# Agent attention and maxout FFN: DMA transposes split in two, head operations with places of their own

## The chip, the cores and the metric

One core of a Trainium2 chip runs the whole kernel. The metric is the device time of one execution in microseconds (us), as a median over runs. A profile of one execution gives the busy time of each engine: PE (TensorE, with its weight loads as PEld), DVE (VectorE), ACT (ScalarE), POOL (GpSimd), and SP (SyncE), which here only issues DMAs.

## The reference

Four batches of 12544 tokens with 128 channels pass through an attention over 49 agents, and what comes out through a feed-forward layer with a maximum of three branches:

```python
a2k = softmax(scale * agents @ k.T)      # 49 x 12544, per batch
agent_v = a2k @ v                        # 49 x 128
q2a = softmax(scale * q @ agents.T)      # 12544 x 49
x = q2a @ agent_v                        # 12544 x 128
h = max(x @ w1, x @ w2, x @ w3)          # 50176 x 768
out = h @ w_out                          # 50176 x 128
```

All inputs and the output are 32-bit floats; the kernel computes in bf16 with 32-bit accumulation.

## The kernel before

**Algebra.** x is never formed. Since x = q2a · agent_v, each branch of the layer is q2a · (agent_v · w). Per batch the kernel computes one matrix G from agent_v: columns C31 hold agent_v·(w3−w1) (for the fifth block of 128 columns, f = FI = 4, w3−w2), columns C21 agent_v·(w2−w1), and the columns from C1O on agent_v·w1·w_out and ones that come with it. The differences of the weights stand in `wall`. With e_q = exp(scale · q · agentsᵀ), a hidden block is relu(e_q·G31) (`relu_first`, L674/677, on ACT), then the maximum of this and e_q·G21 (`max_second`, L685/687, on DVE), and w_out multiplies it on PE (L701) on top of the linear part (L692). The softmax sums are divided out at the end (`out_scale`, L708, DVE).

**Stages.** A row tile has 128 rows. Q is worked in 49 groups of 8 row tiles (s = 0 to 48; the last takes the rests of all four batches). K and V of batch 0 are worked in the head, in 11 groups of 9 tiles (8 in the last); K and V of batch b are worked beside the Q groups of batch b−1, in groups s = 12(b−1)+1 to 12(b−1)+11. Groups 36 to 48 have no K work beside them. At the end of each batch's K work, `k_tail` sums the exponentials (L553), divides (L565/566), multiplies with `wall` (L485) and copies the product from PSUM to G (L574 on DVE, L576 on ACT); this is called the border.

**Turns.** The matmuls want q and k with channels on the partitions, so every tile of them has to be transposed. In the head PE turns k (L365) and DVE copies it (L368). Beside the Q groups, SP turns k by one DMA transpose of all 9 tiles of a group from k_bf to kT (`turn_k`, L502), and q by one DMA transpose of 8 tiles in the groups 12, 24 and 36 to 48 (`turn_by_dma`, L633). In the other Q groups PE turns q (L625) and DVE copies it (L629). GpSimd casts q (L620), k (L494) and v (L498) to bf16 before.

**Order.** Each operation is entered with a number, its place, by `at(key, fn)`, and the sorted list is the program: the order of each engine's instructions is that of the places. A group takes 6 units of place. The tables KEY (steady), LATE (groups from 36 on), OWN (named groups), BORDER (the groups around a border), BATCH0 and BATCH3 (`k_tail`) hold the places. STREAM puts loads, casts and DMA turns 11 units and less ahead of the group that uses them. All loads share 14 buffers (`load_tile`); stores are held back by seven groups, with ten buffers for o_sb. All loads, turns and stores are issued by SP, one after the other.

**The head.** `head` loads K and V tiles of batch 0 in turn; w1 and w3 come (L266) ahead of the last V loads and w2 last, after all of V. `cast_w1` (ACT) and `turn_w1` (L317/318) prepare the linear part, the difference operations (L294) fill `wall`, `warm` (L328) issues matmuls on a unit matrix that nothing reads. `normalise` (L409) makes agent_v from the sums, `product` (L412 to 420) multiplies with C31 of `wall` and copies on ACT, and then with C21 and copies on DVE. The difference C21 is split in two halves of 384 columns, one on DVE and one on GpSimd. `keep_busy` (L788) issues some more unread matmuls in the first groups. w_out is loaded (L270) at the end of the head.

Of the kernel before, what the change touches and what calls it, by code (L numbers as in the profile page):

```python
# [11 lines left out]
AF = mybir.ActivationFunctionType  # L12
# [16 lines left out]
    "s": -2.94209, "ex": -2.10461, "u1": -0.58526, "a1": -0.11108, "u2": 2.13391, "a2": 3.22306,  # L29
    "v1": 3.39126, "u3": 3.76716, "x1": 4.61365, "v2": 4.65907, "u0": 4.68062, "a3": 4.76358,  # L30
    "x2": 4.9054, "a0": 5.15584, "v0": 5.44974, "u4": 5.62746, "x0": 6.09964, "a4": 6.12388,
    "u5": 6.27862, "v3": 6.63325, "a5": 6.82242, "v4": 6.98304, "x4": 6.98433, "lin1": 7.02719,
    "oc12": 7.03328, "sum": 7.23728, "oc10": 7.59283, "x3": 7.74792, "v5": 7.87225, "rec": 8.46283,
    "x5": 9.47889, "oc13": 9.6877, "oc11": 9.69832, "oc14": 10.58762, "oc15": 10.856, "lin0": 10.87306,
    "oc05": 11.17012, "sc1": 11.55345, "oc01": 11.72189, "oc00": 11.77009, "oc03": 11.79963,
    "oc02": 11.90624, "oc04": 11.95959, "sc0": 12.74339, "st": 15.47059,
# [3 lines left out]
        "u2": 0.64554, "u0": 0.6497, "a0": 0.75101, "a2": 0.92875, "sum": 1.27525, "u3": 2.06003,  # L40
        "v0": 2.59116, "x0": 2.68446, "a3": 2.85638, "rec": 2.96325, "u1": 3.03882, "v2": 3.6736,
        "u4": 4.24684, "a1": 4.93475, "x2": 5.01871, "v3": 5.81978, "u5": 5.84299, "a4": 5.908,
        "a5": 6.60823, "x3": 6.61479, "v4": 6.9759, "v5": 7.08557, "x4": 7.15158, "v1": 7.27894,
        "x5": 7.66161, "x1": 7.70792, "lin0": 9.14279, "oc05": 10.43605, "oc00": 10.7932, "oc02": 10.85481,
        "oc03": 11.37967, "oc01": 11.41219, "oc04": 11.66746, "sc0": 11.83826, "lin1": 12.49398,
        "oc10": 12.50239, "oc11": 12.59233, "oc12": 12.77266, "oc13": 12.88978, "oc14": 13.54796,
        "oc15": 13.60373, "sc1": 13.75975, "st": 20.17439,
    },
    1: {
        "qt": -4.60541, "qe": -4.48042, "s": -2.95099, "ex": -1.32724, "ks": 1.62294, "u0": 1.73602,  # L50
        "ke": 2.36058, "sum": 2.56616, "kv": 2.79082, "a0": 2.92319, "ka": 3.26757, "u2": 3.4201,
        "v0": 3.45964, "a2": 3.84717, "u3": 4.22117, "rec": 4.22129, "x0": 4.49406, "a3": 4.56793,
        "u1": 4.62522, "v2": 4.63012, "x2": 4.73195, "a1": 4.86854, "v3": 5.12545, "u4": 5.25359,
        "x3": 5.55542, "ea": 5.62671, "a4": 5.96399, "u5": 6.17953, "a5": 6.26476, "v1": 6.28947,
        "x1": 6.30399, "v4": 6.40498, "v5": 6.63853, "x5": 6.88027, "x4": 7.41578, "lin0": 8.99321,
        "oc00": 9.79175, "oc04": 10.56667, "oc02": 10.75084, "oc03": 11.28772, "oc01": 11.5494,
        "oc05": 11.68913, "sc0": 12.27589, "lin1": 12.53566, "oc13": 12.60573, "oc15": 12.61178,
        "oc10": 12.70709, "oc14": 13.24775, "oc12": 13.54581, "oc11": 13.80424, "sc1": 14.02652,
        "st": 19.02898,
    },  # L60
    34: {
        "qt": -2.58866, "qe": -1.82932, "s": -1.30778, "ex": -1.10174, "ks": 0.14415, "sum": 0.55608,
        "rec": 0.59015, "ke": 0.68278, "u0": 0.7058, "ea": 0.72143, "u2": 1.49989, "a0": 2.15219,
        "v0": 2.18384, "x0": 2.25012, "kv": 2.57078, "a2": 2.84672, "ka": 3.10787, "u3": 3.14749,
        "a3": 3.82134, "u1": 3.94172, "v3": 3.96473, "a1": 4.22804, "x3": 4.34837, "v2": 4.43956,
        "u4": 4.5536, "u5": 4.96643, "a4": 5.32988, "x2": 5.54314, "a5": 6.22364, "v4": 6.22498,
        "v1": 6.372, "x4": 6.51691, "v5": 6.61382, "x1": 6.73976, "x5": 6.95861, "lin1": 8.28778,
        "oc15": 8.36021, "lin0": 8.73553, "oc13": 9.18722, "oc04": 9.72211, "oc14": 10.51955,
        "oc01": 10.73827, "oc02": 10.8464, "oc03": 12.33286, "oc05": 12.39876, "oc00": 12.40014,
        "oc11": 12.72237, "sc0": 13.30654, "oc12": 14.30997, "oc10": 14.62572, "sc1": 14.9543,  # L70
        "st": 25.03309,
    },
    35: {
        "qt": -2.43671, "qe": -1.9414, "s": -1.5744, "ex": -1.28805, "ks": -1.09088, "ke": -0.64495,
        "sum": -0.18909, "kv": -0.10783, "ka": 0.5331, "rec": 0.56684, "u0": 0.82589, "a0": 0.91902,
        "u2": 1.00358, "v0": 1.49877, "x0": 1.58537, "a2": 2.26288, "u3": 2.5102, "v2": 2.57899,
        "x2": 3.98475, "u1": 4.05488, "a3": 4.05504, "v3": 4.37636, "a1": 4.49639, "u5": 4.62208,
        "x3": 4.92789, "a5": 5.44572, "v5": 5.48263, "x5": 5.93851, "u4": 7.30642, "a4": 8.24488,
        "v1": 8.30836, "x1": 8.49394, "lin0": 8.71742, "oc03": 8.91263, "oc02": 9.07857, "v4": 9.24912,
        "x4": 9.32541, "oc00": 9.39236, "oc04": 9.69131, "oc01": 10.88106, "lin1": 10.92225,  # L80
        "oc05": 11.01981, "oc15": 11.13488, "sc0": 11.61665, "oc12": 11.69455, "oc13": 11.87736,
        "oc14": 13.32657, "oc10": 13.37252, "oc11": 13.49981, "sc1": 13.74093, "st": 42.57773,
    },
    36: {
        "s": -4.45673, "ex": -3.49789, "u1": -0.09348, "a1": 2.12897, "u2": 2.20348, "a2": 2.77677,
        "v2": 3.2876, "u0": 3.526, "v1": 3.8727, "x2": 4.34512, "x1": 4.34975, "u3": 4.36198,
        "a0": 4.73186, "a3": 5.00514, "v0": 5.29756, "u4": 5.75498, "x0": 5.91535, "sum": 6.0162,
        "a4": 6.30588, "v3": 6.39331, "x3": 6.48929, "u5": 6.75132, "rec": 7.30888, "a5": 7.33831,
        "v4": 7.78698, "v5": 7.80684, "x5": 7.96407, "x4": 8.12232, "lin1": 9.0675, "oc12": 9.24639,
        "oc14": 9.95322, "oc10": 10.40131, "lin0": 10.43281, "oc04": 10.55626, "oc01": 10.64608,  # L90
        "oc11": 11.24862, "oc15": 12.02168, "oc13": 12.20592, "oc00": 12.38398, "oc03": 12.91102,
        "sc1": 12.98528, "oc02": 14.0029, "oc05": 14.08645, "sc0": 14.96085, "st": 29.7755,
    },
    37: {
        "s": -2.47874, "ex": -1.87009, "u1": -0.70419, "a1": -0.60046, "u2": 2.0221, "a2": 2.21078,
        "v2": 3.56807, "x2": 3.92118, "u0": 4.2218, "v1": 4.32407, "x1": 4.92454, "a0": 5.43373,
        "v0": 5.83985, "u3": 6.06605, "x0": 6.29959, "u5": 6.46966, "v3": 6.48031, "a3": 6.91113,
        "a5": 7.46701, "u4": 7.96938, "sum": 8.00459, "x3": 8.25588, "rec": 8.25634, "v5": 8.35007,
        "lin1": 8.44693, "oc11": 8.49987, "a4": 8.62997, "oc13": 8.8661, "v4": 9.25227, "x5": 9.45205,
        "oc12": 9.91769, "x4": 10.00657, "oc10": 10.0531, "lin0": 10.26202, "oc15": 10.56081,  # L100
        "oc14": 10.87787, "oc04": 10.95601, "oc05": 11.15532, "sc1": 11.49682, "oc01": 11.77199,
        "oc02": 11.78318, "oc00": 11.81904, "oc03": 12.16132, "sc0": 13.17137, "st": 43.83189,
    },
    47: {
        "s": -2.63303, "ex": -1.35705, "u1": -0.72334, "a1": -0.55161, "u2": 2.09887, "a2": 2.6128,
        "v1": 2.71229, "u3": 4.07931, "v2": 4.23837, "a3": 4.51758, "x1": 4.63092, "u0": 4.71212,
        "a0": 5.0718, "x2": 5.13888, "u4": 5.22695, "v0": 5.2509, "x0": 5.96934, "u5": 6.00235,
        "a4": 6.49548, "v3": 6.59342, "v4": 6.61016, "sum": 6.94315, "lin0": 6.95342, "x3": 6.98518,
        "a5": 7.11094, "oc00": 7.22404, "oc02": 7.24709, "v5": 7.29105, "rec": 7.33314, "x4": 7.43763,
        "lin1": 7.62467, "oc03": 7.73819, "oc11": 7.80383, "x5": 7.80889, "oc14": 8.24845, "oc12": 8.30273,  # L110
        "oc04": 8.48507, "oc10": 10.74469, "oc01": 11.20725, "oc05": 11.70935, "sc0": 11.81857,
        "oc15": 11.86159, "oc13": 12.01123, "sc1": 12.03976, "st": 16.08395,
    },
    48: {
        "s": -2.45577, "ex": -1.62439, "u1": -0.82051, "a1": -0.04899, "u2": 1.5047, "v1": 1.68501,
        "a2": 1.84167, "u0": 1.85869, "v2": 2.12726, "a0": 2.96358, "x1": 3.66201, "x2": 3.71048,
# [53 lines left out]
    },  # L170
}
BATCH0 = {
    "red": -0.0796, "tot": 0.34012, "nrm": 0.77389, "p31": 0.90693, "p21": 1.22633,
}
BATCH3 = {
    "red": -1.41636, "tot": -0.09802, "nrm": 0.57786, "p31": 0.95637, "p21": 1.99854,
# [658 lines left out]
```

## Time and profile before

| what | time |
|---|---|
| median of 3 runs | 454.76 us (453.74 to 455.93) |
| the profiled execution | 456.01 us |
| its span (first to last instruction) | 454.2 us |
| PE busy | 433.0 us |
| DVE busy | 404.9 us |
| ACT busy | 398.2 us |
| POOL busy | 169.4 us |
| DMA transposes of k, 9 or 8 tiles | 33, median 1380 ns on SP, 4.1 us to landing |
| DMA transposes of q, 8 tiles | 15, median 1237 ns on SP, 3.1 us to landing |
| first hidden matmul of group 0 (L662) starts | 43.66 us |
| exps of q group 2 start | 58.15 us |
| last output block (L708) starts | 448.64 us |

Times of the trace count from the start of the span. What lies around the span is 1.8 us in the profiled execution. A share of busy time is an average over the head, the batches with K work, and the last 13 groups, which have different limits; therefore the trace is read by stage.

### The profile page before, as it was taken

What the parts mean: (1) busy time and instruction counts of PE and PEld (TensorE: products, weight loads), DVE (VectorE), ACT (ScalarE), POOL (GpSimd) and SP (SyncE); (2) the same over time, 40 slices, a digit from 0 to 9 for tenths busy, and PEclk for the clock granted to TensorE, in tenths of its full rate; (3) what the DMA queues carried; (4) which work ended last, traced back from release to release, by engine and by line L of the source; (5) the groups of instructions that cost most, each with busy time, mean ns of one, the idle gap of its engine ahead of it and who ended that gap; (6) DMA issues with size and microseconds to landing.
All of it is one profiled execution on the core that took longest, in us unless ns stands there. A gap on an engine that the chain in (4) does not pass through costs nothing.

```text
span 454.2 us, 13313 instructions
## 1 busy us (share of the span) xinstructions
PE 433.0 (95%) x5506; PEld 278.0 (61%) x5506; DVE 404.9 (89%) x505; ACT 398.2 (88%) x456; POOL 169.4 (37%) x165
## 2 busy tenths in 40 slices
PE   2878999999999999999999999999999999999995
PEld 2754566666665666666665666666665556565664
DVE  3323899999999999999999999999999999999995
ACT  1655899999999999999988999999988899999983
POOL 4334465555424354465423355554410101011000
PEclk9999999999999999999999999999999999999999
DMA  8998999898879989998899999999667686654933
GB/s 316 412 408 318 258 299 256 282 267 274 226 245 327 289 285 292 304 308 260 250 301 292 293 312 273 308 332 268 185 208 179 183 163 187 175 153 150 348 140 140
DMA packets 83655, 118.86 MB, mean 262 GB/s; under 512 B 57671, under 2 KB 59659, under 8 KB 83595
## 3 DMA queue, kind: packets, MB, share of 16 engines
q1 hardware_dynamic: 83392, 117.92, 86.7%
q8 instruction: 43, 0.70, 0.6%
q14 instruction: 17, 0.14, 0.1%
q10 hardware_dynamic: 203, 0.10, 0.1%
HBM read 78.74 MB, written 25.69 MB: 230 GB/s over the span
## 4 chain that ended last, share of the span: by engine, by line
PE 85%; DMA 8%; DVE 4%; issue 1%; ACT 1%; POOL 0%; DVEq 0%; SPq 0%
PE uv_ps L662 34%; PE o_ps L701 32%; PE o_ps L692 6%; DMA st<-in_k_dram 5%; PE m_ps L639 3%; PE m_ps L625 3%; DVE r L687 2%; DMA st<-in_q_dram 2%; PE m_ps L514 2%; PE m_ps L354 2%; DMA ag_st<-in_agents_dram 1%; PE m_ps L650 1%; PE uv_ps L485 1%; DVE o_sb L708 1%; PE o_ps L788 0%
## 5 line engine op out<-in xcount | busy, mean ns | idle before, releaser
L687 DVE TENSOR_TENSOR r<-uv_ps,a_sb 128x1024 bf16<-128x1024 f32 x245 | 297.5, 1222 | 10.1 <-PE uv_ps L662 5.1
L677 ACT ACTIVATE a_sb<-uv_ps 128x1024 bf16<-128x1024 f32 x245 | 242.9, 1024 | 20.2 <-PE uv_ps L662 17.0
L662 PE MATMUL uv_ps<-e_q,G 49*128 49x512 bf16 (+1 forms) x1248 | 182.5, 369 | 2.5 <-ACT G L420 1.0
L701 PE MATMUL o_ps<-wo_bf,r 128*128 128x128 bf16 x2352 | 179.1, 220 | 0.0
L701 PEld LDWEIGHTS <-r 128*128 128x128 bf16 x2352 | 139.8, 98 | 45.2 <-issue 42.2
L662 PEld LDWEIGHTS <-G 49*128 49x128 bf16 x1248 | 57.2, 93 | 63.4 <-issue 25.4
L620 POOL CAST q_bf<-st 128x1024 bf16<-128x1024 f32 x49 | 50.9, 1040 | 104.1 <-DMA st<-in_q_dram 74.7
L708 DVE TENSOR_TENSOR o_sb<-o_ps,recips 128x512 f32<-128x512 f32 x98 | 67.0, 685 | 2.9 <-PE o_ps L701 1.5
L498 POOL CAST v_bf<-st 128x1152 bf16<-128x1152 f32 (+1 forms) x33 | 37.5, 1137 | 50.3 <-DMA st<-in_v_dram 47.6
L685 ACT ACTIVATE r<-uv_ps 128x1024 bf16<-128x1024 f32 x49 | 50.3, 1026 | 1.3 <-PE uv_ps L662 0.6
L494 POOL CAST k_bf<-st 128x1152 bf16<-128x1152 f32 (+1 forms) x33 | 37.5, 1137 | 35.8 <-DMA st<-in_k_dram 35.7
L674 ACT ACTIVATE uv_ps<-uv_ps 128x1024 f32<-128x1024 f32 x49 | 49.6, 1011 | 0.9 <-PE uv_ps L662 0.6
L526 POOL TENSOR_TENSOR Eacc<-Eacc,e_k 128x441 f32<-128x441 f32 x27 | 27.6, 1024 | 36.2 <-ACT e_k L359 36.2
L692 PE MATMUL o_ps<-G,e_q 128*128 128x256 bf16 x196 | 37.9, 275 | 0.0
L645 ACT ACTIVATE e_q<-m_ps 128x512 bf16<-128x512 f32 x49 | 29.2, 597 | 2.3 <-PE m_ps L639 1.2
L629 DVE COPY qT<-m_ps 128x1024 bf16<-128x1024 bf16 x34 | 23.3, 686 | 3.4 <-PE m_ps L625 3.4
L368 DVE COPY kT<-uv_ps 128x1152 bf16<-128x1152 bf16 (+1 forms) x11 | 8.3, 752 | 17.8 <-PE uv_ps L365 17.8
L692 PEld LDWEIGHTS <-e_q 128*128 128x128 bf16 x196 | 12.1, 97 | 18.3 <-issue 18.1
L625 PE MATMUL m_ps<-ident,q_bf 128*128 128x128 bf16 x272 | 21.2, 222 | 0.2 <-POOL q_bf L620 0.2
L639 PE MATMUL m_ps<-qT,agT 128*64 128x512 bf16 (+1 forms) x104 | 19.9, 389 | 0.6 <-DVE qT L629 0.6
L383 ACT ACTIVATE v_bf<-st 128x1152 bf16<-128x1152 f32 (+1 forms) x11 | 12.2, 1112 | 9.3 <-DMA st<-in_v_dram 9.3
L378 POOL CAST k_bf<-st 128x1152 bf16<-128x1152 f32 (+1 forms) x11 | 12.5, 1137 | 18.3 <-DMA st<-in_k_dram 18.3
(73 smaller groups left out, 231.3 us busy)
## 6 DMA issues: line engine op xcount, KB each, us to landing
st<-in_q_dram SPq DMA_DIRECT2D x48, 512.0 KB, 5.9
out_dram<-o_sb SPq DMA_DIRECT2D x48, 512.0 KB, 5.4
st<-in_k_dram SPq DMA_DIRECT2D x40, 576.0 KB, 5.5
st<-in_v_dram SPq DMA_DIRECT2D x40, 576.0 KB, 8.7
st<-in_k_dram SPq DMA_DIRECT2D x4, 512.0 KB, 4.1
st<-in_v_dram SPq DMA_DIRECT2D x4, 512.0 KB, 6.7
st<-in_moe_w_dram SPq DMA_DIRECT2D x3, 384.0 KB, 11.0
kT<-k_bf SPq DMA_TRANSPOSE x33, 4.1
```

The lines of the kernel that those rows point to most:

```text
L494: nc.gpsimd.tensor_copy(out=d["kb"][:, :n, :], in_=d["k"][:, :n, :])
L498: nc.gpsimd.tensor_copy(out=d["vb"][:, :n, :], in_=d["v"][:, :n, :])
L620: nc.gpsimd.tensor_copy(out=d["qb"], in_=d["q"])
L625: nc.tensor.transpose(t[:, j * P:(j + 1) * P], d["qb"][:, j, :], ident)
L662: nc.tensor.matmul(t[:, h, j0 * P:j1 * P], G[b][h * H:h * H + A, col + f * P:col + (f + 1) * P], d["e"][h * H:h * H + A, j0 * P:j1 * P], s ...
L674: nc.scalar.activation(u, u, AF.Relu)
L677: nc.scalar.activation(a_sb[f], u, AF.Relu)
L685: nc.scalar.activation(r, v_ps[f], AF.Relu)
L687: nc.vector.tensor_tensor(out=r, in0=v_ps[f], in1=a_sb[f], op=ALU.max)
L692: nc.tensor.matmul(t[:, i * 2 * C:(i + 1) * 2 * C], d["e"][:, jj * P:(jj + 1) * P], G[batch[jj]][:, C1O:C1O + 2 * C], start=(i == 0), stop ...
L701: nc.tensor.matmul(t[:, c:c + C], r_sb[f][:, h, jj * P:(jj + 1) * P], wo_bf[:, f, :], start=False, stop=True, skip_group_check=True)
L708: nc.vector.tensor_tensor(out=d["out"][:, j:j + m, :], in0=d["o", o].rearrange("p (j c) -> p j c", c=C), in1=d["r"][:, j:j + m].unsqueeze( ...
```

## The change

Every DMA transpose is issued as two in a row, the first with tile 0 and the second with the rest (tiles 1 to 8, or 1 to 7). In the head, the loads of the weights, the differences, the products and their copies get places of their own in a table HEAD; w2 is loaded in two column parts, 512 to 767 early and 0 to 511 after V; w1 and w3 and the first Q group are loaded earlier in SP's order; the C21 difference of 512 columns is one operation on DVE after `normalise`, and that of the other 256 an earlier one on DVE; w1 is turned after the first hidden matmuls. `product` is divided into the product and its copies, which have places of their own; in `k_tail` the copy on ACT becomes two of 512 columns. The tables LATE, OWN, BORDER, BATCH0 and BATCH3 hold other numbers; KEY and STREAM are unchanged.

```diff
 def turn_k():
     d["kT"] = bf_tile("kT", 3)
-    nc.sync.dma_start_transpose(out=d["kT"][:, :n, :], in_=d["kb"][:, :n, :].rearrange("p j c -> p (j c)"))
+    for j0, j1 in ((0, 1), (1, n)):
+        nc.sync.dma_start_transpose(out=d["kT"][:, j0:j1, :],
+                                    in_=d["kb"][:, j0:j1, :].rearrange("p j c -> p (j c)"))
...
 def turn_by_dma():
     d["qT"] = work.tile([P, GT, P], BF16, tag="qT", bufs=3, name="qT")
-    nc.sync.dma_start_transpose(out=d["qT"], in_=d["qb"].rearrange("p j c -> p (j c)"))
+    for j0, j1 in ((0, 1), (1, n)):
+        nc.sync.dma_start_transpose(out=d["qT"][:, j0:j1, :],
+                                    in_=d["qb"][:, j0:j1, :].rearrange("p j c -> p (j c)"))
...
-def load_w(i):
-    wst[i] = load_tile().rearrange("p j c -> p (j c)")[:, :Dff]
-    nc.sync.dma_start(wst[i], (moe_w1, moe_w2, moe_w3)[i])
+def load_w(i, c0=0, c1=Dff):
+    if i not in wst:
+        wst[i] = load_tile().rearrange("p j c -> p (j c)")[:, :Dff]
+    nc.sync.dma_start(wst[i][:, c0:c1], (moe_w1, moe_w2, moe_w3)[i][:, c0:c1])
...
-def differences_21():
-    difference(nc.vector, C21, 1, 0, slice(0, Dff // 2))
-    difference(nc.gpsimd, C21, 1, 0, slice(Dff // 2, Dff))
+def difference_21(cols):
+    difference(nc.vector, C21, 1, 0, cols)
...
+HEAD = {
+    "wl2": -7.50533, "wl0": -7.40456, "wrm": -6.41713, "wl1": -5.53457, "df": -4.70017,
+    "d31": -3.20784, "w1c": -2.22988, "d21b": -0.89377, "rcp": 2.6689, "wl1b": 3.38798, "nrm": 4.14714,
+    "wol": 4.20207, "d21a": 4.22142, "p31": 4.33884, "p21": 4.35329, "e31a": 4.39759, "e31b": 4.43422,
+    "e21a": 5.11386, "woc": 5.23923, "e21b": 5.27929, "w1t": 6.0631, "pli": 10.9123, "lin": 12.31239,
+}
...
-        at(z + 2.25, cast_w1)
-        at(z + 2.62, turn_w1)
...
+        at(z + HEAD["wl1"], lambda: load_w(1, FI * P, Dff))
+        at(z + HEAD["wl1b"], lambda: load_w(1, 0, FI * P))
+        at(z + HEAD["w1c"], cast_w1)
+        at(z + HEAD["w1t"], turn_w1)
...
+        at(z + HEAD["d21a"], lambda: difference_21(LO))
+        at(z + HEAD["d21b"], lambda: difference_21(slice(FI * P, Dff)))
+        at(z + HEAD["p31"], lambda: product(C31))
+        at(z + HEAD["e31a"], lambda: evacuate(C31, 0, 2 * P))
+        at(z + HEAD["e31b"], lambda: evacuate(C31, 2 * P, Dff))
+        at(z + HEAD["p21"], lambda: product(C21))
...
 (k_tail)
-    at(key + keys["p31"], lambda: product(C31, WC, False))
-    at(key + keys["p21"], lambda: product(C21, C31, True))
+    at(key + keys["p31"], lambda: product(C31, WC))
+    at(key + keys["e31a"], lambda: evacuate(C31, 0, FI * P))
+    at(key + keys["e31b"], lambda: evacuate(C31, FI * P, WC - C31))
+    at(key + keys["p21"], lambda: product(C21, C31))
+    at(key + keys["e21"], lambda: evacuate(C21, 0, Dff))
```

In the order that results, the steady groups are the same on every engine but for the second transpose on SP. In the last groups the order on DVE and ACT is the same, and on PE only the order in which the blocks are accumulated differs. On SP, stores around the borders come after the k load and the turns.

## The prediction

> **What bounds the kernel now.** I read the busy shares of the page first, then its slices and its chain.
>
> ```profile
> PE 433.0 (95%) x5506; PEld 278.0 (61%) x5506; DVE 404.9 (89%) x505; ACT 398.2 (88%) x456; POOL 169.4 (37%) x165
> DVE  3323899999999999999999999999999999999995
> DMA  8998999898879989998899999999667686654933
> PE 85%; DMA 8%; DVE 4%; issue 1%; ACT 1%; POOL 0%; DVEq 0%; SPq 0%
> ```
>
> PE carries the chain; DMA heads it (8%), which is the opening. I then cut the span into stages with the table of windows; columns: stretch, length, busy time and count of PE, weight load, DVE, ACT, POOL, clock, DMA share, GB/s.
>
> ```profile
> 44.00:47.50 3.50, 3.50 (x32) 2.13 (x30) 1.24 (x3) 1.94 (x2) 1.72 (x2) 0.52 0.90 63
> 60.04:68.19 8.15, 8.15 (x112) 5.42 (x108) 8.12 (x11) 7.81 (x10) 5.35 (x6) 1.00 1.02 261
> 151.00:224.00 73.00, 72.80 (x965) 47.84 (x963) 71.63 (x90) 69.39 (x82) 37.01 (x36) 1.00 1.01 286
> 254.00:325.00 71.00, 70.80 (x937) 46.65 (x937) 69.83 (x87) 67.54 (x79) 37.03 (x35) 1.00 1.03 287
> ```
>
> In one steady group PE is busy 8.15 of 8.15 us and DVE 8.12: two engines are full, so no order of work gains there. In the two middle batches the 16 DMA engines are full as well (1.01 and 1.03); counting stretches without a packet in flight I find 0.10 and 0.00 us there, against 1.84 us in 60 to 124. Gains can come only from where engines stand still: the step from head to steady work, the borders, the end. The timeline of the step (start, duration, engine, line; in brackets the idle time before and its releaser):
>
> ```profile
> 39.88 0.63 ACT L383 ACTIVATE v_bf<-st 128x512 bf16<-128x512 f32 x1 [1.56 <-DMA st<-in_v_dram]
> ...
> 41.06 0.41 PE L639 MATMUL m_ps<-qT,agT 128*64 128x512 bf16 x2 [0.55 <-DVE qT L629]
> ...
> 41.40 0.38 PE L405 MATMUL m_ps<-e_k,v_bf 128*128 128x49 bf16 x8
> 41.92 0.20 DVE L409 TENSOR_TENSOR avT<-m_ps,k_recip 128x49 bf16<-128x49 f32 x1
> 42.18 0.52 PE L485 MATMUL uv_ps<-wall,avT 128*64 128x512 bf16 x4 [0.40 <-DVE avT L409]
> 42.73 0.87 ACT L420 ACTIVATE G<-uv_ps 128x256 bf16<-128x256 f32 x2 [0.63 <-PE uv_ps L485]
> ...
> 43.66 0.77 PE L662 MATMUL uv_ps<-e_q,G 49*128 49x512 bf16 x4 [0.97 <-ACT G L420]
> 45.26 1.02 DVE L418 CAST G<-uv_ps 128x256 bf16<-128x256 f32 x2 [2.67 <-PE uv_ps L485]
> 47.70 1.02 ACT L677 ACTIVATE a_sb<-uv_ps 128x1024 bf16<-128x1024 f32 x1 [1.29 <-PE uv_ps L662]
> ```
>
> The last v tile lands at 39.80 and its cast ends at 40.51, but the values' matmuls (L405) start only at 41.40, behind the scores of q group 0, which wait for DVE's copy of qT. DVE stands idle 2.67 us before it copies the second half of G; ACT loses its last 1.29 us before 47.70. From there ACT has no gap until the exps of group 2 at 58.15.
>
> **What the Trainium skill says.** "Perfetto Trace Analysis", section "DMA Instruction — HWDGE (DVE, Sync)": the profiled time of such an issue is the wait for a lock, the generation of descriptors and the push of a semaphore; the movement is not in it. The trace agrees (columns: count, shortest/median/longest ns, first and last start):
>
> ```profile
> L502 SPq DMA_TRANSPOSE kT<-k_bf x33: 1237/1380/2132, 43.6 to 320.3; - x33
> ...
> DMA to landing us min/median/max: 3.0/4.1/6.1
> ```
>
> SP is held 1.24 to 1.38 us, the data lands 3.0 us or later after the start. The qT transposes take 1237 ns with 8 tiles, the shortest kT of 9 tiles 1248: the issue hardly grows with size. "DMA: Bandwidth & Descriptors", section "Rules for kernel authors", says that under 64 KB a transfer is mostly overhead; one tile is 32 KB, and before has no transpose so small. "TensorE: Matmul & The Clock Gate", section "What's actually happening", says that an idle window of about 3.4 us halves the clock; here it is 0.52 in 44.0 to 47.5, after a sparse PE. "SBUF — State Buffer", section "Who interferes with whom", says that DVE and GpSimd lock each other out of a shared port. The trace agrees: the normalising multiply (L566) took 0.21 us at 136.14, but 0.87 at 236.09, beside a k cast of GpSimd from 235.75 to 236.89.
>
> **The change part by part.** *Head loads.* In SP's list q0, w1 and w3 move up by several loads, and the 0.131 MB of w2's columns 512 to 767 go ahead of the last v tiles. The arrays were ahead of the last v before, so what it newly waits for is that part: 0.131 MB at the head's 0.59 MB per 1.43 us is +0.32, landing 40.12. The other 0.26 MB of w2 still follow the last v.
>
> *Step to steady work.* Cast 0.63 from 40.20 (0.08 after landing, as before): values at about 40.85, since q0's turn is now done earlier; 41.40 before, so −0.55. avT ends at 41.57 instead of 42.12. The product C31 (0.52) and C21 (0.85 seen at 44.36 at clock 0.52, so 0.44 at full) follow each other; C21's operand is a 512-column difference on DVE (0.54 measured for 384, scaled to about 0.65) after avT; GpSimd's half of it is gone. So u0 starts at 42.9 to 43.3 instead of 43.66, G's C21 half is ready near 44.1 instead of 46.28, and v0 starts near 44.8 instead of 47.18. ACT's 1.29 and part of its earlier waits close: 1.7 to 2.1 us at most. But the next thing is late: q group 2. Its load is issued at 47.52, lands 53.46, and its PE turn is at 55.68, after a cast of 1.04: 1.12 us of slack. That load starts behind the first kT transpose (43.61), w_out and k, by SP's order, so it won't move up with the step; what the step gains above 1.12 is lost there.
>
> *Split of the turns.* 33 kT and 15 qT issues become 96: 48 more on SP. A one-tile issue is bounded below by a plain load's 0.33 and above by 1.24, the 8-tile issue. I take 0.6 for what it adds where nothing covers it, as the smaller data may shorten the rest. Behind the first pair are queued w_out, k2, q2, v2; so q2's 1.12 becomes 0.5. Step: about **−0.5** (ends +0.2 and −2.1). w1's six transposes and their copy on DVE move behind u0 and u2; DVE's G copies (1.02) ahead of v0 hide the former, its wait for v0 the latter; uncovered, both would cost about 1 us, which the +0.2 end doesn't hold but the range does. The differences of columns done between the head's kT copies fill DVE time of which the slices show two thirds free.
>
> *Steady groups.* SP issues k, q, out, v and a turn, 0.33 to 1.4 each, some 3.1 of 8.15 us, so 1.24 more isn't a bound for SP. Cover is the slack of loads: q, v and kT are ready 7.2 us or more before use in the two middle batches. Over the ten turns that follow before the border gives time back, that covers 0.72 us of lost DMA time per group. The engines have no idle time there, so a second issue which loses less movement costs **0**; at 1.2 it costs up to 10 × 0.48 = 4.8 us a batch, in two batches. Below zero: a first tile that lands sooner gains nothing, as qT lies ready 5 us ahead. I take 0.
>
> *Borders.* Exps of q come every 8.15 us, but 10.21 at each of the first two borders: 1.8 us too much at the first, 2.6 with its neighbours at the second. The reduction, reciprocal and G copies on DVE fill most; POOL's cast beside L566 cost 0.66 there once. After has new places there; stores move behind the k load and turns, hidden as long as o_sb's ten buffers last (a store was held seven groups), and the first copy into Eacc moves ahead of a q cast on GpSimd, which is 37% busy; ACT's G evacuation of 1024 becomes two of 512, 0.6 each beside 1.0, +0.2 per border on an engine that has room. I take **−0.6** in all (ends +1.0, −2).
>
> *Later tables and the end.* In the last groups only the places of matmuls move; the order on DVE and ACT stays. The last stages, e_q at 433.3 to end 454.2, keep their work: **−0.1** (ends ±0.5).
>
> Sum −1.2. The profiled execution was 456.01 us, 454.2 of it span; −1.2 gives 454.8. The median of the three runs is 454.76, 1.25 below the profiled one: the forecast for runs is 453.6.
>
> **Rivals.** *Slower: the transposes take the DMA.* Each one-tile transpose costs a full second generation, 1.2 us, in which no data of that queue moves. For: the issue doesn't grow with tiles, and there is no idle time in the middle batches. Against: earlier loads may still be moving meanwhile. It decides at 0.72 us per group; at 1.2 the bound is 9.6 us for both batches, of which I take two thirds, as a generation that overlaps a load in flight loses less: 453.6 + 6.4 = 460.0. Then GpSimd's casts wait for loads, and PE for them. *No change:* q2's landing eats the step's gain, as SP pays 1.1 us or more ahead of it, and DVE stays full at the borders: about 454.8. For: slack of just 1.12. *Faster:* the full 2.0 at the step, if q2 lands in time, 0.7 at border 2 and three hiccups of 0.36 in the steady period: −3.8, 451. Against: all of it needs q2 earlier by 0.9.
>
> **How the numbers follow.** 0.5%, about what a measurement of this kernel can tell from no change, is 2.27 us: 452.5 and 457.0. Chances: small gain 0.42 (own range 452.6 to 454.5), no change 0.12, slower by the DMA 0.25, faster 0.21. Of the likeliest 0.02 spills over the faster bound, and of slower 0.02 stays within it; some 0.02 goes to larger losses of the small-gain case. Faster 0.23, same 0.52, slower 0.25. Range: 450.8, the faster case's middle, to 460.0, the DMA's price: it leaves out about 0.1 on each side.
>
> **What would show it.** Right: u0 at 43 to 43.4, ACT without its gap near 47.7, exps of group 2 at 57.4 to 57.8, turns in pairs with the first short, border intervals near 9.9, no new waits on k or q loads after 150. Wrong: a first turn of a pair as long as the second with idle DMA engines behind it, waits of POOL's casts on loads that end in waits of PE, exps of group 2 later than 58.15, or border intervals above 10.2.

## The result: 480.7 us, slower by 5.8%

| | median us | lowest to highest | ratio to before, 95% interval |
|---|---|---|---|
| before | 455.19 | 453.74 to 455.93 | |
| after | 480.72 | 479.29 to 485.25 | 1.0582 [1.0504, 1.0659] |

The forecast was 453.6, range 450.8 to 460.0: wrong by 27 us, and outside the range. Medians and ratios in this document are of runs in the faster of the chip's two states; one run of the split in before, at 485.09 us, lay in the slower one and is left out. The profiled execution of after took 485.25 us, 483.5 of it span.

The page of after (busy time; slices of DVE and DMA; the chain by engine and by line):

```profile
PE 439.1 (91%) x5506; PEld 275.6 (57%) x5506; DVE 407.5 (84%) x506; ACT 399.2 (83%) x459; POOL 168.8 (35%) x164
...
DVE  3135899999988988899979999989788898889876
...
DMA  8998878888759797997979999997774656544593
...
DMA 44%; SPq 19%; PE 18%; POOL 9%; DVE 4%; issue 3%; ACT 2%; POOLq 0%; DVEq 0%; ACTq 0%
DMA st<-in_k_dram 24%; DMA st<-in_q_dram 13%; SPq L523 12%; PE uv_ps L691 6%; PE o_ps L730 6%; SPq L661 5%; POOL k_bf L514 5%; POOL q_bf L647 3%; DVE r L716 3%; DMA st<-in_moe_w_dram 2%; DMA kT<-k_bf 2%; DMA qT<-q_bf 1%; PE o_ps L721 1%; PE uv_ps L339 1%; DMA ag_st<-in_agents_dram 1%
```

The busy times are nearly those of before: no work was added on the engines that compute. The chain changed altogether. PE had 85% of it; now it runs through k and q loads (37%), the issue of turns on SP (17%) and the casts on GpSimd (8%). By stage, in the table of windows (columns as in the prediction), after:

```profile
60.00:124.00 64.00, 64.00 (x851) 42.16 (x848) 63.24 (x80) 61.01 (x72) 33.77 (x32) 1.00 0.81 239
151.00:224.00 73.00, 68.42 (x880) 43.09 (x879) 66.10 (x82) 64.35 (x75) 34.28 (x33) 1.00 0.93 277
254.00:335.00 81.00, 78.44 (x1015) 50.17 (x1014) 76.27 (x95) 73.89 (x86) 39.55 (x37) 1.00 0.98 286
375.00:430.00 55.00, 50.75 (x544) 28.98 (x544) 48.34 (x53) 48.39 (x53) 7.30 (x7) 1.00 0.56 156
```

and the late groups of before:

```profile
375.00:430.00 55.00, 55.00 (x596) 32.28 (x592) 52.02 (x57) 53.06 (x58) 7.28 (x7) 1.00 0.65 204
```

In 60 to 124 PE stays full. Later it has gaps in every stage, and in the late groups too, where the DMA engines are busy only 0.56 of the time. So there they are not what runs out. The start of the exps of some q groups shows where the time went:

| exps of q group | before | after | behind |
|---|---|---|---|
| 2 (head done) | 58.1 | 58.7 | 0.6 |
| 13 (first border past) | 149.8 | 152.7 | 2.9 |
| 25 (second border past) | 250.2 | 262.0 | 11.8 |
| 37 (third border past) | 348.7 | 369.9 | 21.2 |
| 48 (last) | 433.3 | 460.7 | 27.4 |
| end of span | 454.2 | 483.5 | 29.3 |

The stretch of the chain between 400 and 420 us in after, where there is only q work (start, duration, what; L661 is `turn_by_dma`, L647 the q cast of after):

```profile
406.10 1.62 SPq L661
407.71 0.05 issue
407.76 4.65 DMA st<-in_q_dram
...
412.56 1.05 POOL q_bf L647
413.61 0.02 issue
413.63 1.12 SPq L661
414.75 0.04 issue
414.79 1.29 SPq L661
416.08 0.04 issue
416.13 4.64 DMA st<-in_q_dram
```

This is a loop. SP works through its list in order. The next q load stands behind the turns of the group before it; the turns wait for the cast; the cast waits for the load. One round: two issues and gaps 2.50, load 4.65, cast with gaps 1.22, together 8.37 (the round from 404.92 to 413.63 took 8.71, as one of its issues was 1.62 long). PE needs 7.71. Over the late groups of after the medians are 4.5 for the load and 8.3 for the interval from turn to turn; in before they are 4.6 and 7.0, under PE's 7.71. In the K groups of the second batch of after (151 to 224): 1.11 + 1.30 + 0.09 for the issues, 4.91 for the k load, 1.22 for the cast, 8.63 together, and the measured median interval is 8.65, over the 8.15 that PE and DVE need. There a part of the second issue came back, because the k loads landed sooner (KB each, median us to landing, in 151 to 224; before, then after):

```profile
st<-in_k_dram SPq DMA_DIRECT2D x7, 576.0 KB, 5.4
```

```profile
st<-in_k_dram SPq DMA_DIRECT2D x8, 576.0 KB, 4.9
```

Added up the same way, with 1.38 for its one issue and 5.4 for the load, the round of before is about 8.0 us there, close under 8.15; this is an estimate from these medians.

### The profile page after: what moved, and what is told of

It is laid out like the page before. It is cut to its first block, busy times and chain, and to the rows that moved or that the text cites. A ratio compares the mean times of both kernels' runs of the same rounds, so it can differ in the third digit from the quotient of the medians.

```text
span 483.5 us, 13371 instructions
## 1 busy us (share of the span) xinstructions
PE 439.1 (91%) x5506; PEld 275.6 (57%) x5506; DVE 407.5 (84%) x506; ACT 399.2 (83%) x459; POOL 168.8 (35%) x164
## 4 chain that ended last, share of the span: by engine, by line
DMA 44%; SPq 19%; PE 18%; POOL 9%; DVE 4%; issue 3%; ACT 2%; POOLq 0%; DVEq 0%; ACTq 0%
DMA st<-in_k_dram 24%; DMA st<-in_q_dram 13%; SPq L523 12%; PE uv_ps L691 6%; PE o_ps L730 6%; SPq L661 5%; POOL k_bf L514 5%; POOL q_bf L647 3%; DVE r L716 3%; DMA st<-in_moe_w_dram 2%; DMA kT<-k_bf 2%; DMA qT<-q_bf 1%; PE o_ps L721 1%; PE uv_ps L339 1%; DMA ag_st<-in_agents_dram 1%
## 5 line engine op out<-in xcount | busy, mean ns | idle before, releaser
L647 POOL CAST q_bf<-st 128x1024 bf16<-128x1024 f32 x49 | 51.1, 1042 | 113.4 <-DMA st<-in_q_dram 95.8
L691 PEld LDWEIGHTS <-G 49*128 49x128 bf16 x1248 | 53.8, 94 | 59.8 <-issue 23.2
L514 POOL CAST k_bf<-st 128x1152 bf16<-128x1152 f32 (+1 forms) x33 | 37.5, 1136 | 89.7 <-DMA st<-in_k_dram 89.7
L674 ACT ACTIVATE e_q<-m_ps 128x512 bf16<-128x512 f32 x49 | 29.3, 598 | 10.9 <-PE m_ps L668 9.3
L548 POOL TENSOR_TENSOR Eacc<-Eacc,e_k 128x441 f32<-128x441 f32 x27 | 27.6, 1024 | 0.0
L721 PEld LDWEIGHTS <-e_q 128*128 128x128 bf16 x196 | 11.8, 97 | 22.5 <-issue 21.9
L370 ACT ACTIVATE e_k<-m_ps 128x441 bf16<-128x441 f32 (+1 forms) x33 | 17.8, 539 | 8.1 <-PE m_ps L679 7.1
L365 PEld LDWEIGHTS <-kT 128*128 128x128 bf16 x392 | 15.3, 99 | 15.4 <-DVE kT L379 7.9
L370 ACT ACTIVATE e_k<-uv_ps 128x441 bf16<-128x441 f32 (+1 forms) x11 | 5.9, 538 | 20.9 <-PE uv_ps L365 20.9
```

Source lines behind the costliest of these rows:

```text
L514: nc.gpsimd.tensor_copy(out=d["kb"][:, :n, :], in_=d["k"][:, :n, :])
L647: nc.gpsimd.tensor_copy(out=d["qb"], in_=d["q"])
L691: nc.tensor.matmul(t[:, h, j0 * P:j1 * P], G[b][h * H:h * H + A, col + f * P:col + (f + 1) * P], d["e"][h * H:h * H + A, j0 * P:j1 * P], s ...
L721: nc.tensor.matmul(t[:, i * 2 * C:(i + 1) * 2 * C], d["e"][:, jj * P:(jj + 1) * P], G[batch[jj]][:, C1O:C1O + 2 * C], start=(i == 0), stop ...
```

## The experiments

Loop theory: SP's order chains load, cast, turn and next load; a second issue lengthens every round by its whole length. Rivals: the second transpose costs DMA time (as the prediction's slower case had it); the new places cost the time; a second transpose is dear in some other way.

**One turn again.** After with the single transpose back in both places:

```diff
-    for j0, j1 in ((0, 1), (1, n)):
-        nc.sync.dma_start_transpose(out=d["kT"][:, j0:j1, :],
-                                    in_=d["kb"][:, j0:j1, :].rearrange("p j c -> p (j c)"))
+    nc.sync.dma_start_transpose(out=d["kT"][:, :n, :], in_=d["kb"][:, :n, :].rearrange("p j c -> p (j c)"))
```

and the same for qT.

> After with each DMA turn as one transpose again; places, head and w2's two parts stay. Loop theory (a load, its cast, the turn on SP, then the next load: a second issue of 1.29 us lengthens that chain by its full length in every group): the loss of 25 us goes, 454 to 456, late groups at 7.71 us. Places theory (the head, border and end tables cost most of it): still 465 or more, with late groups at 8.3. The head's own loss, seen as u0 at 45.66 against 43.66 and exps of group 2 at 58.7 against 58.15, should stay and cost about 0.5 us.

Measured 455.73 us, ratio to before 1.0021 [1.0008, 1.0034]. K groups at 8.15, late groups at 7.71. The split carries all of the loss that can be told from noise, but for 0.2%. The head's delay stayed, and larger: the first hidden matmul started at 46.01, exps of group 2 at 59.1. Between group 2 and group 48 this kernel took 373.6 us, before 375.2: the new places win 1.6 us in this trace.

**Two turns in before.** The same edit, the other way round, in before.

> Before with nothing but the split of the turns. Loop theory: 477 to 481; groups of batch 1 keep 8.15 us (the ready data covers), those of the next two batches take 8.6 to 8.9, the late ones 8.3 against 7.71. Theory that the DMA engines' time is the limit: late groups stay at 7.71, as the engines are busy 0.65 there, and the whole stays under 466. Places theory: 455 to 457.

Measured 481.28 us, 1.0567 [1.0497, 1.0636]. Late groups took 8.3. The batches were less even than expected: in its profiled execution the first border took 5.3 us more, after which the second batch ran at 8.15, and the third fell to 8.7 to 9.4 in its second half. I read it so that a stall puts ready data back in stock, which is then used up again; no run shows this by itself. The total was at the upper end of what I expected.

**The second turn behind the next loads.** Before, with the split, but

```diff
 at(key + keys["kt"], turn_k)
+at(key + keys["kt"] + 4.52, turn_k_rest)
...
 at(key + K["kt"], turn_by_dma)
+at(key + K["kt"] + (4.52 if s > LAST else 0.0), turn_by_dma_rest)
```

`turn_k` and `turn_by_dma` issue tile 0, the new functions the rest.

> Before with the same split, but the second transpose of each group stands in SP's list behind the next group's k and q loads (in the late groups behind the next q load); in groups 12, 24 and 36 both stay together. As many issues, packets and bytes as with the split alone. Loop theory: the chain holds only one issue (1.11 us) again, so 454 to 458, late groups at 7.71. Theory that each transpose costs DMA time or SP time as such: as slow as the split alone, 470 or more.

Measured 461.45 us, 1.0136 [1.0110, 1.0162]: better than the split by 20 us, but over the expectation. The intervals between groups tell why: the exps of group 2 started at 63.9 (58.1 in before), and all groups from then on had the intervals of before, 8.15 and 7.71. The table of waits has the one place:

```profile
PE m_ps L354 <- DMA kT<-k_bf: 6.0, 1, 6.0
```

In the first K group the data is needed soon after it is turned, and the rest of kT came too late by one wait. So I kept both turns together in K groups 1 and 2:

```diff
-at(key + keys["kt"] + 4.52, turn_k_rest)
+at(key + keys["kt"] + (4.52 if s > 2 else 0.0), turn_k_rest)
```

> As the run with the second turn behind the next loads, but K groups 1 and 2 keep both turns together, so that no scores wait 6 us for kT at the start. All 96 transposes are there. The 8 us of that wait go: 454.5 to 456. If something else in that run cost the 6 us, still 458 or more.

Measured 459.64 us, 1.0096 [1.0069, 1.0124], over the expectation again: the wait moved to K group 3, now the first with a late second turn, and the exps of the next q group came 12.33 us after those before instead of 8.15. That 4.2 us is nearly the whole difference of 4.6. The other intervals between groups are those of before, so elsewhere the 96 transposes cost nothing.

**Loads one group ahead.** After, with both turns, and one line changed:

```diff
-STREAM = {"kl": 0.0, "ld": 0.5, "kc": 1.0, "qc": 1.5, "vl": 1.9, "kt": 2.0, "vc": 3.2}
+STREAM = {"kl": -6.0, "ld": -5.5, "kc": 1.0, "qc": 1.5, "vl": -4.1, "kt": 2.0, "vc": 3.2}
```

> After unchanged but for the loads of k, q and v, which stand one group (6 units of place) earlier, so that a load no longer waits behind the turn of the group before it. Loop theory: one chain now spans two groups, 8.3 to 8.8 us for two, so it no longer limits: 454 to 457 with all 96 transposes. Theory that the second transpose costs DMA time: no gain in the middle batches, 470 or more; that it costs SP time: no gain either.

Measured 455.69 us, 1.0010 [0.9998, 1.0021]: 25 us back with all 96 transposes in place, at DMA shares of 1.03 and 1.02 in 151 to 224 and 254 to 325. The waits of SP's queue (line, releaser, total us, times, longest), for before, after and this kernel:

```profile
SPq L502 <- POOL q_bf L620: 156.5, 27, 8.8
SPq L633 <- POOL q_bf L620: 72.9, 15, 7.7
```

```profile
SPq L523 <- POOL k_bf L514: 98.3, 26, 5.3
SPq L661 <- POOL q_bf L647: 67.1, 15, 5.1
```

```profile
SPq L523 <- POOL q_bf L647: 108.5, 26, 6.1
...
SPq L661 <- PE m_ps L668: 29.4, 9, 4.6
```

In before and after SP's q turns wait for casts, 15 times of 15. With the loads ahead nine of their fourteen waits are for PE, which has to give back a qT buffer: the stream of data is ahead of PE, not behind it. This separates the theories: neither DMA time nor SP time as such was short.

**Only q, only k.** Before with only the q turns split:

> Before with only the 15 q turns split; the 33 k turns stay single. Loop theory: the batches with K work keep 8.15 us, each late group goes from 7.71 to 8.3 (7.1 for the chain with one issue, and 1.2 for the second), so some 12 groups by 0.6: 461 to 463. DMA time theory: 455 to 456, as the engines have spare time in the late groups.

Measured 460.28 us, 1.0109 [1.0077, 1.0141]. The K groups kept 8.15; the late groups took between 7.7 and 9.2, half of them 8.3 to 8.5. Slightly under the expectation.

Before with only the k turns split:

> Before with only the 33 k turns split, q turns single. The split of all costs 27.6 us, that of q 5.3; if the two add up, 455 + 22 = 477, late groups at 7.71, groups of the last two K batches at 8.5 to 8.9, batch 1 at 8.15 once its stock of ready data lasts.

Measured 472.71 us, 1.0373 [1.0339, 1.0408]; all late groups at 7.71. The parts are 5.3 and 17.7, together 23.0, where the split of both costs 26.1 (the expectation reckoned with 27.6). The intervals of the three ratios, of 3.2, 1.6 and 1.5 us to either side, leave open whether the parts simply add up.

**Holding SP without a second turn.** Before, single turns, and behind each q turn two (then four) loads that nothing reads:

```diff
+for _ in range(2):
+    nc.sync.dma_start(work.tile([1, 8], FP32, tag="dummy", bufs=8, name="dummy"), q[0, 0:1, 0:8])
```

> Before with single turns, and behind each of the 15 q turns two loads of 32 bytes that nothing reads (some 0.5 us each on SP). Loop theory: what counts is only how long SP is held before the next q load, so the late period becomes about 7.1 + 1.0 = 8.1 us and the whole 459 to 460. Theory that a second transpose as such is dear: no change, 455.

Measured 455.74 us, 1.0013 [0.9995, 1.0031]: no loss, so the expectation failed. SP's queue there:

```profile
387.53 1.24 SPq L633 DMA_TRANSPOSE qT<-q_bf  x1
388.82 0.73 SPq L635 DMA_DIRECT2D dummy<-in_q_dram  x2
389.60 0.36 SPq L616 DMA_DIRECT2D st<-in_q_dram  x1
...
394.93 1.24 SPq L633 DMA_TRANSPOSE qT<-q_bf  x1
```

The two loads held SP 0.73 us, not 1.0. The q load behind them took 0.36 us to issue instead of 0.58, and its cast began 4.40 us after that issue, against 4.65 in before (medians of eleven late rounds), so a part of the hold came back. The round shown is 7.40; the median is 7.5, against 7.0 in before. So the round did grow, and it stayed under PE's 7.71: that fits the loop theory, whose forecast of 8.1 was too high. But a run without a loss leaves open whether holding time counts at all, or only a second turn's data ahead of the load. Four loads:

> Before with single turns and four loads of 32 bytes behind each q turn, which hold SP for 1.45 us (4 by 0.36), more than the 1.2 to 1.3 of a second q turn. Theory that SP's holding time sets the chain: late groups 8.3 or more, as with the split of the q turns alone (460.3), so 460 to 462. Theory that the next load is delayed by the second turn's place in the queue of data (its data moves only after its own issue, and the load's data behind it): the hold is largely spent while the first turn's data moves, next q load lands 3.5 to 4 us after its issue instead of 4.4, intervals of q turns 7.2 to 7.8, total 455 to 457.

Measured 461.45 us, 1.0150 [1.0094, 1.0206], near the 460.28 of the split of q alone, but with a wide spread, 459.82 to 465.25:

```profile
373.07 1.24 SPq L633 DMA_TRANSPOSE qT<-q_bf  x1
374.36 1.32 SPq L635 DMA_DIRECT2D dummy<-in_q_dram  x4
375.73 0.36 SPq L616 DMA_DIRECT2D st<-in_q_dram  x1
...
381.05 1.52 SPq L633 DMA_TRANSPOSE qT<-q_bf  x1
```

For comparison the split of q alone:

```profile
391.54 2.47 SPq L634 DMA_TRANSPOSE qT<-q_bf  x2
394.06 0.58 SPq L616 DMA_DIRECT2D st<-in_q_dram  x1
...
400.13 2.47 SPq L634 DMA_TRANSPOSE qT<-q_bf  x2
```

The rounds shown are 7.98 in the one and 8.59 in the other. Over the last twelve q turns the profiles give (us; the round is the median interval from turn to turn, PE needs 7.71):

| kernel | start of the turn to start of the next q load | round | exps of group 37 to exps of group 48 |
|---|---|---|---|
| second turn behind the next load | 1.2 | 6.5 | 84.64 |
| before | 1.3 | 7.0 | 84.65 |
| two small loads | 2.1 | 7.5 | 84.65 |
| q turns split | 2.5 | 8.5 | 90.79 |
| after | 2.5 | 8.3 | 90.87 |
| four small loads | 2.7 | 8.2 | 90.45 |

The round follows the time on SP ahead of the next load, whatever fills that time: four loads of 128 bytes in all lengthen it about as much as a second transpose does. As long as the round is under 7.71 nothing is lost, and over it the late groups lose about 6 us. The size of the last line's loss is less sure than its round. Two of its groups took 10.29 us, beside a q load that landed only after 6.25 us, and they make 5.2 of its 5.8 us; why that load was late is open.

**What the parts that were not to blame are worth.** Before with only the loads ahead:

> Before with its loads of k, q and v one group earlier in SP's list, single turns. Loop theory: the chain of 7.1 to 7.4 us was already under the period, so little is won: 453.5 to 455.5, at most the hiccup at 239.9 (0.4 us) and what q group 2 loses. If loads were a bound of before in the middle batches, 452 or less.

Measured 455.45 us, 1.0007 [0.9992, 1.0023]: loads were no bound of before. Then with the new places of after for the borders, late groups and end, and its copies of G in `k_tail`, but the head and the first groups of before, first with the loads ahead:

> The head and first groups of before, the new border, late and end places and evacuations of after, single turns, loads one group ahead. With the head of after the new places gave 1.6 us back between group 2 and group 48 (59.1 to 432.7 against 58.1 to 433.3); with before's head that gain should stay in the total: 453 to 454. If the gain came from the head's delay itself (more data ready), 455.

Measured 455.15 us, 1.0002 [0.9988, 1.0016]: no gain that can be told. And with the loads where before has them:

> Before's head and first groups, after's new border, late and end places and evacuations, single turns, loads where before has them. The new places save about 1.3 us between group 2 and group 48 in the traces: 453.5 to 455, the fastest of all; if the median of before is not beaten by 0.3%, the places are worth nothing that can be told.

Measured 453.59 us, 0.9979 [0.9962, 0.9996]: the lowest of all, 0.2% under before. The 0.3% that I had asked for is just reached by the medians (455.06 for before beside it) and not by the ratio; its profile, of a slower execution, shows no gain between group 2 and group 48 (375.1 us against 375.2). Against it, after with one turn, which has the same places and the new head, stands at 1.0021 [1.0008, 1.0034]. The two differ in the head and the first groups alone, by 0.42% of the ratios, about 1.9 us; the intervals leave room for anything from 0.1 to 0.7%. So the new head costs something. With the loads ahead as well the gain of the places can't be told; 0.2% is the most that these runs suggest for them, and it is not shown.

## Why the prediction was wrong, by its steps

**What bounds the kernel.** That PE and DVE fill the steady groups was right: in every run without the loop they took 8.15 and 7.71 us again. What I left out is the view of waits of SP's own queue, shown above: already in before each of the 15 q turns waited for a cast. I looked at how long data lies ready ahead of PE, not at how fast the stream that makes it ready can run.

**The split.** This is the step that failed: "Cover is the slack of loads" and "a second issue which loses less movement costs 0". The lasting cover of a stream that runs in rounds is not its stock but the room between its round and PE's, 7.71 − 6.99 = 0.7 us in the late groups by the medians. I had the number 0.72 as a threshold, but for lost DMA time and from stock spread over ten turns: that the two agree is chance. I took 0.6 for the issue of one tile; the row of after (count, shortest/median/longest ns) has

```profile
L523 SPq DMA_TRANSPOSE kT<-k_bf x66: 1113/1301/2837, 43.6 to 347.3; - x66
...
DMA to landing us min/median/max: 2.2/3.3/5.5
```

so 1.11 us for one tile. The rest behind it, seven or eight tiles, takes 1.30 by the median, and a q pair holds SP for 2.45 us where one turn of eight tiles held it for 1.24: 1.2 us more, near my upper bound. With that the round goes over PE's period in the late groups and in the second and third batch of K work; in the first (60 to 124) it is about equal, 8.2 us between turns by the median. For the late groups, with DMA engines a third idle, I put nothing at all; they lost 6.2 us. What the Trainium skill says under "DMA Instruction — HWDGE (DVE, Sync)" in "Perfetto Trace Analysis", that this time is generation on the issuing side and not movement, agrees with 1.11 us for 32 KB against 1.24 for 256 KB: the time hardly grows with the bytes. I read from it that SP has room (4.3 of 8.15 us), which is true of its sum and says nothing of its order.

**The slower rival** had the side and the price of an issue right (1.2 us), and its mechanism wrong. "No data of that queue moves" would not have been cured by the loads ahead, nor by the second turn behind the next loads; both were. Hence its 460 was 21 short: it counted two batches less their stock, and not the late groups, nor the borders. Of the signs of being wrong, late exps of group 2 (58.7) and long border intervals (11.4 and 10.9 us) came; first turns as long as the second did not (1.11 against 1.30).

**The step to steady work.** Predicted −0.5, measured +0.6 in after and +0.9 with one turn, at the exps of group 2. It is more than the spread of profiles: those of kernels with the head of before have this point between 56.7 and 58.3 (but for the one with its long wait, 63.9), the three with the new head at 58.7, 59.1 and 59.5. The last v landed at 40.20 (40.12 predicted), but values did not follow it. The timeline of after:

```profile
40.35 0.62 POOL L396 CAST v_bf<-st 128x512 bf16<-128x512 f32 x1 [4.55 <-PE uv_ps L339]
...
40.62 0.50 ACT L370 ACTIVATE e_k<-uv_ps 128x392 bf16<-128x392 f32 x1 [0.83 <-PE uv_ps L365]
41.02 1.16 ACT L394 ACTIVATE v_bf<-st 128x1152 bf16<-128x1152 f32 x1
42.07 0.59 ACT L674 ACTIVATE e_q<-m_ps 128x512 bf16<-128x512 f32 x1
42.55 0.63 ACT L394 ACTIVATE v_bf<-st 128x512 bf16<-128x512 f32 x1
...
43.57 1.04 POOL L647 CAST q_bf<-st 128x1024 bf16<-128x1024 f32 x1
...
43.65 0.21 DVE L420 TENSOR_TENSOR avT<-m_ps,k_recip 128x49 bf16<-128x49 f32 x1 [1.08 <-PE m_ps L416]
43.77 1.38 DVE L306 TENSOR_TENSOR wall<-st 128x512 bf16<-128x512 f32 x1
...
45.21 0.52 PE L505 MATMUL uv_ps<-wall,avT 128*64 128x512 bf16 x4 [0.70 <-DVE wall L306]
45.66 0.61 PE L691 MATMUL uv_ps<-e_q,G 49*128 49x512 bf16 x4
```

The 1.3 MB of q0, w1 and w3 that moved ahead delayed not the last v but the k loads: the last k landed at 34.61 instead of 30.88. Its turn and its scores on PE then each stood behind four of the unread matmuls (1.02 us), and its exps came at 40.62 (35.12 before); two casts of v and the exps of q queued behind them on ACT, and the last values matmuls started at 43.23 (41.40 before). I had followed one load, and not each that the moved ones pass. The difference of 512 columns took 1.38 us and not 0.65, from 43.77 on, beside a q cast of GpSimd from 43.57 to 44.61, and PE waited 0.70 us for it. "SBUF — State Buffer" of the Trainium skill, section "Who interferes with whom", names a lock between the two engines for operations that read two inputs from SBUF, and the numbers agree with it. With one turn the same two operations came one after the other, and the difference took what I had put:

```profile
43.64 1.04 POOL L645 CAST q_bf<-st 128x1024 bf16<-128x1024 f32 x1
...
44.80 0.68 DVE L306 TENSOR_TENSOR wall<-st 128x512 bf16<-128x512 f32 x1
```

There u0 was late all the same (46.01), as the last values matmuls started only at 44.25; so the late values (1.8 us in after) weigh more than the lock. In after u0 started at 45.66 where I had 42.9 to 43.3. That q group 2 would eat a gain could not be seen, as there was no gain.

**Borders and end.** Predicted −0.7; with one turn the stretch from group 2 to 48 was 1.6 shorter. Three single groups of before that took 8.51, 8.57 and 8.51 us instead of 8.15 make 1.1 of it; they are absent there, but also in the profile with four small loads, which has the places of before. What is left for the borders is about 0.5, near the forecast in one trace, and not to be told in the medians.

## What to carry to other kernels

Look for loops that close through an in-order issuing queue: load, cast, something issued that waits for the cast, and next load behind it. Add up one round from the trace and set it against the period of the bound engine; the difference is what an added issue may take in every round without loss, however idle the DMA engines are; data in stock covers more only until it is used up. If a round is near the period, put the next loads ahead of the waiting issue before anything else is changed there.

## What was not expected of the hardware

In these runs a DMA transpose of one tile of 32 KB held SP for 1.11 us, and one of eight tiles for 1.24; the one tile landed at the earliest 2.2 us after its issue started, the eight 3.0. So splitting a turn nearly doubles its issue, 2.45 us in place of 1.24. And a q load right behind a transpose took 0.58 us to issue, behind small loads 0.36, so that 0.73 us of other issues lengthened the round by only 0.5.
